# The first attention batch of a fused attention and MLP kernel: two squares a unit on GpSimd, QK and transposes interleaved singly, Z and PV of unit 2 summed beside its exponentials

## Chip, cores, metric

One core of a Trainium2 chip. The metric is the device time of one execution in microseconds (us), as the median of several runs. The rounds ran on different chips; a ratio always compares a kernel with the kernel before in the same rounds. A profile is one execution; its span is 1.7 to 1.9 us shorter than the device time of the same run.

## The reference, cut to what matters

```python
# q, k, v: [8 batches, 12 heads, 448, 64] float32
def rmsnorm(x, g):
    return x / np.sqrt(np.mean(x * x, axis=-1, keepdims=True) + 1e-06) * g
scores = np.matmul(rmsnorm(q, g_q), rmsnorm(k, g_k).transpose(0, 1, 3, 2)) / np.sqrt(64)
attn = softmax(scores)                      # with the row maximum taken off
x = heads_side_by_side(np.matmul(attn, v))  # [3584, 768]
h = x @ w_in                                # [768, 2048]
out = np.maximum(0.01 * h, h) @ w_out       # [2048, 768]
```

## The kernel before

The work is cut into 24 units of four heads; three units make a batch. Each unit goes through the same steps:

- squares of q and k (`prep_sq` on ScalarE or `prep_sqp` on GpSimd), their sums (`prep_ssq`, VectorE), 1/rms as Ln and Exp (`prep_rinv`, ScalarE), the norm (`prep_norm`, VectorE) and the transposes (`prep_tr`, TensorE with a copy by VectorE);
- scores S^T for seven key tiles (`qk`), the first of which gives the shift of the exponent (`shift_max` on VectorE, `shift_mm` on TensorE and VectorE), and seven exponentials (`ex`, ScalarE);
- Z, the sum of the exponentials (`zsum`), and PV (`pv`), 28 matmuls each, then 1/Z as Ln and Exp (`zinv`) and their product (`xmul`).

The MLP of a batch (`moe1`, `moe2`) needs all three units. It waits in a queue, from which `fill` takes work for TensorE between the later units' steps. So from unit 3 on there is MLP work to fill TensorE with; in units 0 to 2 there is none. The parts that the change touches:

```python
def zsum(u):
    s = st[u]
    s["zt"] = slot()
    for t in range(NS):                       # 7 key tiles, 4 matmuls each
        for r in range(2):
            for a in range(2):
                nc.tensor.matmul(s["zt"][64 * a:64 * a + 64, r, 0:S], ones16[64 * r:64 * r + 64],
                                 s["et"][64 * r:64 * r + 64, t, a], start=(t == 0), stop=(t == NS - 1))
# pv(u): the same loop with v for ones16, into two banks
# ... cut ...
for u in range(3):
    ex(u)
    if u == 0:
        prep_ssq(1)
    prep_rinv(u + 1)
    if u > 0:
        zinv(u - 1)
    prep_sq(u + 2, ALL, (0 if u == 0 else 1,))
    prep_norm(u + 1)
    if u > 0:
        xmul(u - 1)
    # ... loads cut ...
    prep_qg(u + 2, nc.gpsimd)
    prep_sqp(u + 3, (0,))
    qk(u, STEPS[1]); ex(u)
    prep_ssq(u + 2)
    if u == 0:
        qk(u, STEPS[2]); ex(u); qk(u, STEPS[3]); ex(u)
        for ti in range(2):
            prep_tr(u + 1, ti, VV)
        score0(u + 1); shift_max(u + 1)
    else:
        for ti in range(2):
            prep_tr(u + 1, ti, VV)
        qk(u, STEPS[2]); ex(u)
        score0(u + 1); shift_max(u + 1)
        qk(u, STEPS[3]); ex(u)
    shift_mm(u + 1)
    zsum(u)
    pv(u)
```

The softmax here doesn't subtract the row's maximum and nothing guards it: scores larger than these inputs give would overflow.

## Time and profile before

| | before |
|---|---|
| median | 459.26 us (459.0 to 459.46, 3 runs) |
| span of the profile | 458.0 us |
| TensorE busy to 55.9 us | 35.7 of 55.9 us |
| TensorE busy after it | 396.2 of 402.1 us |

Two lines of the page of the kernel before: busy time by engine, with the share of the span, and the clock granted to TensorE in 40 slices of 11.45 us, in tenths of full speed.

```profile
PE 431.9 (94%) x3840; PEld 223.5 (49%) x3840; DVE 205.9 (45%) x320; ACT 314.4 (69%) x446; POOL 95.9 (21%) x74
...
PEclk9567899999999999999999999999999999999999
```

The first line says that TensorE is the busy engine, but it averages two stages. The second marks the stage in which it is not: slices 2 to 5 have a reduced clock, and in the same slices TensorE's own row, which opens the prediction, reads only 4, 6, 7 and 6 tenths busy. An array at half clock is called cold below, one at full clock warm.

### The profile page before, as it was taken

How to read it: one execution, taken by the hardware profiler on the slowest of the kernel's cores; microseconds unless marked ns; L12 is line 12 of the kernel's file. 1: busy time of each engine (PE TensorE's matmuls, PEld its weight loads, DVE VectorE, ACT ScalarE, POOL GpSimd, SP SyncE). 2: the span in 40 equal slices, each digit the busy share in tenths (PEclk: the TensorE clock that was granted, in tenths of full speed). 3: DMA queues.
4: the chain of work that ended last, by engine and by line, in shares of the span. 5: the costliest groups of instructions: out<-in, count | busy, mean ns of one | idle time of the engine just before them, and what ended most of it. 6: DMA issues, size and time to landing. Idle time of an engine off the chain costs nothing.

```text
span 458.0 us, 8922 instructions
## 1 busy us (share of the span) xinstructions
PE 431.9 (94%) x3840; PEld 223.5 (49%) x3840; DVE 205.9 (45%) x320; ACT 314.4 (69%) x446; POOL 95.9 (21%) x74
## 2 busy tenths in 40 slices
PE   7467699999999999999999999999999999999995
PEld 6133244554445544554455544554455544555563
DVE  3766564555434733645434634654444631311021
ACT  4858688768876679858876679767876678544300
POOL 3954331330230330331130330331130200000000
PEclk9567899999999999999999999999999999999999
DMA  8999997545625734644644733654633330021022
GB/s 283 191 236 228 163 225 152 134 97 157 142 43 161 182 73 106 142 97 147 142 74 138 176 76 101 142 106 139 142 55 76 76 76 0 2 70 36 0 69 70
DMA packets 62508, 54.13 MB, mean 118 GB/s; under 512 B 36868, under 2 KB 57348, under 8 KB 62468
## 3 DMA queue, kind: packets, MB, share of 16 engines
q1 hardware_dynamic: 52192, 41.76, 33.6%
q0 software_dynamic: 10272, 11.80, 17.1%
q8 instruction: 30, 0.49, 0.4%
q14 instruction: 10, 0.08, 0.0%
q10 hardware_dynamic: 4, 0.00, 0.0%
HBM read 45.61 MB, written 11.01 MB: 124 GB/s over the span
## 4 chain that ended last, share of the span: by engine, by line
PE 88%; ACT 5%; DVE 4%; DMA 1%; issue 1%; ACTq 0%; DVEq 0%
PE op L280 32%; PE hps L265 31%; PE sT L235 8%; PE sT L175 8%; PE pv L250 7%; ACT et L194 3%; DVE ssq L135 1%; PE warm L350 1%; PE pb L219 1%; DVE pm L207 1%; PE tp L155 1%; ACT gt L267 1%; DMA grow<-in_g_k_dram 1%; DVE qkT L156 1%; ACT sq L122 1%; DVE xt L259 1%
## 5 line engine op out<-in xcount | busy, mean ns | idle before, releaser
L194 ACT ACTIVATE et<-sT,eb 128x896 f16<-128x896 f32 x165 | 158.0, 1009 | 37.6 <-PE sT L175 35.0
L265 PE MATMUL hps<-xt,win 128*128 128x448 f16 x768 | 153.1, 353 | 0.8 <-ACT et L192 0.8
L280 PE MATMUL op<-wout,gt 128*128 128x384 f16 x896 | 153.3, 326 | 0.0
L280 PEld LDWEIGHTS <-gt 128*128 128x128 f16 x896 | 84.6, 98 | 63.3 <-issue 10.9
L130 POOL TENSOR_TENSOR qg<-rq,ggb 128x896 f32<-128x896 f32 (+2 forms) x25 | 63.9, 2559 | 236.5 <-DVE n L147 232.3
L265 PEld LDWEIGHTS <-win 128*128 128x128 f16 x768 | 72.2, 98 | 75.0 <-issue 10.9
L267 ACT ACTIVATE gt<-hps 128x448 f16<-128x448 f32 x128 | 65.6, 548 | 25.2 <-PE hps L265 24.6
L284 DVE COPY ost<-op 128x384 f32<-128x384 f32 x56 | 31.0, 556 | 89.9 <-PE op L280 89.8
L147 DVE TENSOR_TENSOR n<-qg,rinv 128x896 f16<-128x896 f32 (+2 forms) x25 | 26.5, 1063 | 81.9 <-ACT rinv L141 44.2
L175 PE MATMUL sT<-qkT 64*64 64x448 f16 x660 | 51.6, 370 | 7.5 <-ACT et L194 6.8
L135 DVE TENSOR_REDUCE ssq<-sq 128x14 f32<-128x896 f32 (+2 forms) x49 | 49.9, 1059 | 5.1 <-ACT sq L122 5.1
L241 ACT ACTIVATE rz<-sT 128x896 f32<-128x896 f32 x24 | 22.0, 917 | 42.0 <-PE sT L235 42.0
L235 PE MATMUL sT<-et,ones 64*64 64x448 f16 x672 | 39.9, 378 | 0.6 <-ACT et L194 0.5
L250 PE MATMUL pv<-et,vt 64*64 64x448 f16 x672 | 37.9, 363 | 0.0
L175 PEld LDWEIGHTS <-qkT 64*64 64x64 f16 x672 | 14.5, 106 | 45.9 <-issue 38.9
L259 DVE TENSOR_TENSOR xt<-pv,rz 128x448 f16<-128x448 f32 x48 | 27.7, 619 | 9.7 <-ACT rz L242 8.6
L212 DVE TENSOR_REDUCE sT<-sT 128x1 f32<-128x896 f32 x21 | 23.0, 1096 | 19.6 <-PE sT L175 19.5
L235 PEld LDWEIGHTS <-ones 64*64 64x64 f16 x672 | 20.6, 113 | 16.1 <-issue 7.4
L250 PEld LDWEIGHTS <-vt 64*64 64x64 f16 x672 | 20.9, 112 | 13.5 <-issue 2.7
L147 DVE TENSOR_TENSOR n<-rk,rinv 128x896 f16<-128x896 f32 (+2 forms) x25 | 26.2, 1047 | 0.0
L242 ACT ACTIVATE rz<-rz 128x896 f32<-128x896 f32 x24 | 22.8, 949 | 0.8
L122 ACT ACTIVATE sq<-rk 128x896 f32<-128x896 f32 x23 | 21.6, 940 | 0.2 <-DMA rk<-in_k_dram 0.2
(48 smaller groups left out, 136.4 us busy)
## 6 DMA issues: line engine op xcount, KB each, us to landing
rq<-in_q_dram SPq DMA_DIRECT2D x24, 448.0 KB, 6.2
rk<-in_k_dram SPq DMA_DIRECT2D x24, 448.0 KB, 6.4
out_dram<-ost SPq DMA_DIRECT2D x56, 192.0 KB, 2.7
vt<-in_v_dram POOLq DMA_DIRECT2D x24, 224.0 KB, 6.0
win<-in_moe_w_in_dram POOLq DMA_DIRECT2D x8, 384.0 KB, 12.3
wout<-in_moe_w_out_dram POOLq DMA_DIRECT2D x2, 1536.0 KB, 18.4
qkT<-n SPq DMA_TRANSPOSE x19, 4.0
grow<-in_g_q_dram ACTq DMA_DIRECT2D x1, 0.2 KB
```

The lines of the kernel that those rows point to most:

```text
L130: eng.tensor_tensor(buf(u, "qg")[:, :, c[0]:c[1]], raw[u][0][:, :, c[0]:c[1]], ggb[:, None, None, :].broadcast_to([P, 2, n, D]), op=ALU.mult)
L135: nc.vector.tensor_reduce(buf(u, "ssq")[:, ti, :, c[0]:c[1]], buf(u, "sq")[:, ti, :, c[0]:c[1]], axis=AXL.X, op=ALU.add)
L147: nc.vector.tensor_tensor(buf(u, "n16")[:, ti, c[0]:c[1]].rearrange("p s a d -> p a s d"), src[:, :, c[0]:c[1]], buf(u, "rinv")[:, ti, :, ...
L175: nc.tensor.matmul(banks[a][64 * r:64 * r + 64, 0:S].rearrange("p (t x) -> p t x", t=NS), kT(u, r, a, t), qT(u, r, a), start=True, stop=True)
L194: nc.scalar.activation(s["et"][:, t], sT[:, :, 0:S], AF.Exp, bias=s["eb"], scale=1.0)
L235: nc.tensor.matmul(s["zt"][64 * a:64 * a + 64, r, 0:S], ones16[64 * r:64 * r + 64], s["et"][64 * r:64 * r + 64, t, a], start=(t == 0), sto ...
L250: nc.tensor.matmul(s["pv"][r][64 * a:64 * a + 64, 0:S], vts[u % NV][64 * r:64 * r + 64, a, t], s["et"][64 * r:64 * r + 64, t, a], start=(t ...
L259: nc.vector.tensor_tensor(xts[b][:, g, r], s["pv"][r][:, 0:S], s["rz"][:, r], op=ALU.mult)
L265: nc.tensor.matmul(hps[:, 0:S], win16[:, kt // 2, kt % 2, ts(ft, P)], xt[:, kt // 2, kt % 2], start=(kt == 0), stop=(kt == KT - 1))
L267: nc.scalar.activation(gt[:, ft, ds(S * (b % 2), S)], hps[:, 0:S], AF.Prelu, bias=0.0, scale=1.0, alpha=0.01)
L280: nc.tensor.matmul(op2[:, 0:HC], gt[:, ft, ts(t, P)], wout16[:, ft, ds(HC * half, HC)], start=(ft == 0), stop=(ft == FT - 1))
L284: nc.vector.tensor_copy(ost[0][:, ds(HC * half, HC)], op2[:, 0:HC])
```

## The change

The intent is to shorten the first batch, in which TensorE waits, so that the stage which it saturates starts earlier. The diff, cut to its core (left out are the new arguments of `zsum`, `zinv` and `pv`, calls moved with them, the square of unit 5 that leaves ScalarE, and the load of the output weights, now issued in unit 1 instead of unit 2):

```diff
-        for x in range(20): warm-up matmul
+        warm(32)                                   # before the product of the two gains
         ...
-        vcopy(ggb, gps[:, 0:D])
-        for x in range(44): warm-up matmul
+        warm(28)
         ...
+        acopy(ggb, gps[:, 0:D])
         ...
+        prep_sq(1, ALL, (0,))                      # ahead of unit 0's copies on ScalarE
         ...
+        prep_ssq(1, ALL, (0,))                     # ahead of unit 0's maximum on VectorE
         qk(0, STEPS[0])
-        prep_sq(1)
+        prep_sq(1, ALL, (1,))
 
         for u in range(3):
+            n = u + 1
             ex(u)
             if u == 0:
-                prep_ssq(1)
+                prep_ssq(n, ALL, (1,))
             ...
-            prep_sq(u + 2, ALL, (0 if u == 0 else 1,))
             ...
-            prep_sqp(u + 3, (0,))
+            prep_sqp(u + 3)                        # both squares on GpSimd
             ...
             ex(u)
-            prep_ssq(u + 2)
-            ... (u == 0: QK 3 to 6, then both transposes; else transposes, QK 3, 4, shift, QK 5, 6)
-            shift_mm(u + 1)
-            zsum(u)
-            pv(u)
+            if u > 0:
+                prep_tr(n, 0, VV)
+                prep_tr(n, 1, VV)
+                xmul(u - 1)
+            qk(u, STEPS[2])
+            ex(u)
+            if u == 0:
+                prep_tr(n, 0, VV)
+            qk(u, (5,))
+            ex(u)
+            if u == 0:
+                prep_tr(n, 1, VV)
+                qk(u, (6,)); ex(u); prep_sq(2, ALL, (0,)); score0(n); shift_max(n); shift_mm(n)
+            elif u == 1:
+                score0(n); shift_max(n); qk(u, (6,)); ex(u); shift_mm(n)
+            else:
+                qk(u, (6,)); ex(u)
+            if u < 2:
+                zsum_slot(u); pv(u)
+                prep_ssq(u + 2)                    # now behind the shift
+            else:
+                prep_ssq(u + 2)
+                st[u]["zt"] = [aux([P, 512], FP32, "zt") for r in range(2)]
+                zsum(u, 0, 5)                      # while exponentials 5 and 6 run
+                pv(u, 0, 5)
+                qk(n, STEPS[0])
+                zsum(u, 5, NS)
+                pv(u, 5, NS)
+                zinv(u)                            # in two halves
+                shift_max(n)
+                xmul(u)
+                push_moe1(0); push_moe2(0); queue.pop(0)[1]()
+                shift_mm(n)
+                ex(n)
```

More of the change, by code (lines that the diff above doesn't have):

```diff
@@ L227, with zsum, zsum_slot @@
     xts = {}
-    def zsum(u):
+    def zsum(u, t0=0, t1=NS):
         s = st[u]
-        s["zt"] = slot()
-        for t in range(NS):
+        for t in range(t0, t1):
             for r in range(2):
                 for a in range(2):
-                    nc.tensor.matmul(s["zt"][64 * a:64 * a + 64, r, 0:S], ones16[64 * r:64 * r + 64],
+                    nc.tensor.matmul(s["zt"][r][64 * a:64 * a + 64, 0:S], ones16[64 * r:64 * r + 64],
                                      s["et"][64 * r:64 * r + 64, t, a], start=(t == 0), stop=(t == NS - 1))
+    def zsum_slot(u):
+        s = st[u]
+        s["zslot"] = slot()
+        s["zt"] = [s["zslot"][:, r] for r in range(2)]
+        zsum(u)
     def zinv(u):
@@ L240, in zinv, with pv @@
         s["rz"] = zpool.tile([P, 2, S], FP32, tag="rz", name="rz")
-        nc.scalar.activation(s["rz"], s["zt"][:, :, 0:S], AF.Ln)
-        nc.scalar.activation(s["rz"], s["rz"], AF.Exp, bias=0.0, scale=-1.0)
-    def pv(u):
+        if "zslot" in s:
+            nc.scalar.activation(s["rz"], s["zslot"][:, :, 0:S], AF.Ln)
+            nc.scalar.activation(s["rz"], s["rz"], AF.Exp, bias=0.0, scale=-1.0)
+        else:
+            for r in range(2):
+                nc.scalar.activation(s["rz"][:, r], s["zt"][r][:, 0:S], AF.Ln)
+                nc.scalar.activation(s["rz"][:, r], s["rz"][:, r], AF.Exp, bias=0.0, scale=-1.0)
+    def pv(u, t0=0, t1=NS):
         s = st[u]
-        s["pv"] = [aux([P, 512], FP32, "pv") for r in range(2)]
-        for t in range(NS):
+        if t0 == 0:
+            s["pv"] = [aux([P, 512], FP32, "pv") for r in range(2)]
+        for t in range(t0, t1):
             for r in range(2):
@@ L328, with warm @@
     VV = ((ALL, vcopy),)
-    def attend(u):
-        zsum(u)
-        pv(u)
-        zinv(u)
+    def warm(n):
+        for x in range(n):
+            nc.tensor.matmul(wbank[:, 0:P], onesp, onesp, start=True, stop=True)
     with tc.manual_schedule():
@@ L341 @@
         load(2)
+        gps = aux([P, 512], FP32, "gps")
+        wbank = aux([P, 512], FP32, "warm")
+        warm(32)
         nc.vector.scalar_tensor_tensor(grow[:, 0], grow[:, 0], 0.125, grow[:, 1], op0=ALU.mult, op1=ALU.mult)
-        gps = aux([P, 512], FP32, "gps")
-        warm = aux([P, 512], FP32, "warm")
-        for x in range(20):
-            nc.tensor.matmul(warm[:, 0:P], onesp, onesp, start=True, stop=True)
         nc.tensor.matmul(gps[:, 0:D], one32, grow[:, 0], start=True, stop=True)
-        vcopy(ggb, gps[:, 0:D])
-        for x in range(44):
-            nc.tensor.matmul(warm[:, 0:P], onesp, onesp, start=True, stop=True)
+        warm(28)
         prep_sq(0, CA, (0,))
         prep_sq(0, CB, (0,))
+        acopy(ggb, gps[:, 0:D])
         prep_sq(0, ALL, (1,))
@@ L366 @@
         prep_norm(0, K0, (1,))
+        prep_norm(0, K1, (1,))
         tpk = aux([P, NS, P], FP16, "tp")
@@ L374 @@
         trk(K0, vcopy)
-        prep_norm(0, K1, (1,))
+        prep_ssq(1, ALL, (0,))
         qk(0, STEPS[0])
-        prep_sq(1)
+        prep_sq(1, ALL, (1,))
         trk(K1, acopy)
@@ L388 @@
         for u in range(3):
+            n = u + 1
             ex(u)
             if u == 0:
-                prep_ssq(1)
-            prep_rinv(u + 1)
+                prep_ssq(n, ALL, (1,))
+            prep_rinv(n)
             if u > 0:
                 zinv(u - 1)
-            prep_sq(u + 2, ALL, (0 if u == 0 else 1,))
-            prep_norm(u + 1)
-            if u > 0:
-                xmul(u - 1)
+            prep_norm(n)
             load(u + 4)
-            gate(u + 1)
+            gate(n)
             prep_qg(u + 2, nc.gpsimd)
-            prep_sqp(u + 3, (0,))
+            prep_sqp(u + 3)
             load_v(u + 3)
@@ L405 @@
                 load_w_in(1024, 1024)
-            if u == 2:
+            if u == 1:
                 for f in range(2):
@@ L410 @@
             ex(u)
-            prep_ssq(u + 2)
-            if u == 0:
-                qk(u, STEPS[2])
-                ex(u)
-                qk(u, STEPS[3])
+            if u > 0:
[4 more added lines that the diff above has]
+            ex(u)
+            if u == 0:
+                prep_tr(n, 0, VV)
[3 more added lines that the diff above has]
+                prep_tr(n, 1, VV)
+                qk(u, (6,))
+                ex(u)
+                prep_sq(2, ALL, (0,))
+                score0(n)
+                shift_max(n)
+                shift_mm(n)
+            elif u == 1:
+                score0(n)
+                shift_max(n)
+                qk(u, (6,))
@@ L416 @@
                 ex(u)
-                for ti in range(2):
-                    prep_tr(u + 1, ti, VV)
-                score0(u + 1)
-                shift_max(u + 1)
-            else:
-                for ti in range(2):
-                    prep_tr(u + 1, ti, VV)
-                qk(u, STEPS[2])
+                shift_mm(n)
+            else:
+                qk(u, (6,))
                 ex(u)
-                score0(u + 1)
-                shift_max(u + 1)
-                qk(u, STEPS[3])
-                ex(u)
@@ L430 @@
-            shift_mm(u + 1)
-            zsum(u)
-            pv(u)
+            if u < 2:
+                zsum_slot(u)
+                pv(u)
+                prep_ssq(u + 2)
[8 more added lines that the diff above has]
+                zinv(u)
+                shift_max(n)
+                xmul(u)
+                push_moe1(0)
+                push_moe2(0)
+                queue.pop(0)[1]()
+                shift_mm(n)
+                ex(n)
@@ L434 @@
         for u in range(3, NU):
             for d in range(4):
-                if u > 3 or d > 0:
+                if d > 0 or u > 3:
                     qk(u, STEPS[d])
-                if d == 0 and u > 3:
-                    shift_max(u)
-                    zsum(u - 1)
-                    pv(u - 1)
-                    shift_mm(u)
-                    zinv(u - 1)
-                if u == 3 and d == 0:
-                    zinv(u - 1)
-                ex(u)
+                    if d == 0:
+                        shift_max(u)
+                        zsum_slot(u - 1)
+                        pv(u - 1)
+                        shift_mm(u)
+                        zinv(u - 1)
+                    ex(u)
@@ L447 @@
                 if d == 0:
-                    xmul(u - 1)
                     if u == 3:
-                        push_moe1(0)
-                        push_moe2(0)
                         prep_rinv(4)
@@ L454 @@
                         gate(4)
+                    else:
+                        xmul(u - 1)
                     if u + 4 < NU:
@@ L468 @@
                         prep_tr(4, ti, VV)
-                    prep_sq(5, ALL, (1,))
                 if u + 2 < NU:
@@ L477 @@
                 fill(u, d)
-        attend(NU - 1)
+        zsum_slot(NU - 1)
+        pv(NU - 1)
+        zinv(NU - 1)
         xmul(NU - 1)
```

## The prediction

> **What bounds the kernel now.** I read the page's rows of busy tenths first, to find out where the span is lost, then the busy time by stretch, then the waits and the timeline of the stretch that loses.
>
> ```profile
> PE   7467699999999999999999999999999999999995
> ACT  4858688768876679858876679767876678544300
> ```
>
> A slice is 11.45 us. TensorE is saturated from the sixth slice on and ragged in the first five. Busy time by stretch, cut where the clock changes, puts numbers on that (columns after the length: PE, PEld, DVE, ACT, POOL busy, then the clock granted):
>
> ```profile
> 13.30:30.10 16.80, 9.23 (x80) 3.99 (x83) 10.77 (x19) 10.25 (x17) 13.21 (x15) 0.50 0.98 216
> 30.10:36.90 6.80, 4.12 (x70) 2.26 (x63) 6.02 (x9) 6.28 (x8) 4.59 (x4) 0.99 1.15 225
> 36.90:43.80 6.90, 5.50 (x63) 2.64 (x65) 3.83 (x8) 5.76 (x9) 0.71 (x2) 0.51 0.96 219
> 43.80:50.70 6.90, 3.19 (x51) 1.66 (x47) 5.81 (x10) 5.79 (x7) 5.64 (x5) 0.99 0.75 180
> 50.70:54.00 3.30, 3.30 (x40) 1.58 (x44) 0.46 (x2) 0.67 (x2) 0.00 (x0) 0.50 0.95 143
> 55.90:110.00 54.10, 53.23 (x489) 26.84 (x488) 30.27 (x44) 43.25 (x63) 13.62 (x9) 1.00 0.77 166
> 110.00:458.00 348.00, 342.96 (x2973) 175.68 (x2969) 141.77 (x216) 233.47 (x332) 52.71 (x29) 1.00 0.40 94
> ```
>
> From 55.9 us on, PE is idle for 0.9 + 5.0 us of 402, most of it the tail. So the span is about "time of the first MLP matmul" plus 402 us of TensorE work that the diff leaves alone. What the change can gain is an earlier start of that saturated stage. Before it, nothing is saturated: the limit is one chain that goes round ScalarE, VectorE and TensorE. ScalarE's timeline shows its holes:
>
> ```profile
> 14.54 1.01 ACT L194 ACTIVATE et<-sT,eb 128x896 f16<-128x896 f32 x1 [0.50 <-DVE eb L222]
> 16.52 0.32 ACT L140 ACTIVATE uu<-ssq,eps_t 128x28 f32<-128x28 f32 x1 [0.98 <-DVE ssq L135]
> 17.00 0.93 ACT L122 ACTIVATE sq<-rq 128x896 f32<-128x896 f32 x1
> 17.84 5.48 ACT L194 ACTIVATE et<-sT,eb 128x896 f16<-128x896 f32 x6
> 27.77 1.16 ACT L192 ACTIVATE et<-s,eb 128x448 f16<-128x448 f32 x2 [4.44 <-DVE eb L222]
> 39.13 1.16 ACT L192 ACTIVATE et<-s,eb 128x448 f16<-128x448 f32 x2 [0.46 <-DVE eb L222]
> 48.93 1.91 ACT L194 ACTIVATE et<-sT,eb 128x896 f16<-128x896 f32 x2 [1.03 <-PE sT L175]
> 53.46 0.92 ACT L241 ACTIVATE rz<-sT 128x896 f32<-128x896 f32 x1 [2.63 <-PE sT L235]
> ```
>
> First exponentials of units 0, 1, 2 start at 14.54, 27.77, 39.13; unit 3's at 55.27. The 4.44 us hole is unit 1's shift: in unit 0 the transposes of unit 1 come after the last QK, so copies, score tile and maximum run while ScalarE has nothing left. The 2.63 us hole is Z of unit 2, started only after unit 3's shift, on a cold array. TensorE's side of that end:
>
> ```profile
> 50.60 2.81 PE L235 MATMUL sT<-et,ones 64*64 64x448 f16 x28
> 53.20 1.93 PE L250 MATMUL pv<-et,vt 64*64 64x448 f16 x28
> 55.94 3.57 PE L265 MATMUL hps<-xt,win 128*128 128x448 f16 x18 [0.81 <-ACT et L192]
> ```
>
> 28 Z matmuls take 2.81 us here and 1.5 us at full clock (68.9 us).
>
> **What the Trainium skill says.** "GPSIMD Engine Reference", section 4.1, calls GpSimd about 2x slower than VectorE on two-input elementwise work. The trace agrees in kind: a square of 128x896 takes 1.67 us there against 0.94 on ScalarE. It matters only if GpSimd's row fills up. "TensorE: Matmul & The Clock Gate", Part 1, says that the clock is halved or full, judged over free-running windows of about 3.4 us. The trace agrees: 0.50 and 1.00, with changes near 30.1, 36.9, 43.8, 50.7 and 54.0, all multiples of 3.4 us apart. The same part says that ScalarE's and VectorE's queues are strictly in order; hence a reduction placed behind a shift waits for it even if its data came early. No run here tests that by itself.
>
> **The change part by part.** I carry the chain forward with the durations of the trace: square on ScalarE 0.94, sum of squares on VectorE 1.04, rinv pair 0.58, exponential 0.92 start to start, norm pair 2.18, tp copy 0.6, Ln+Exp of Z 1.87, shift from the score tile to the bias 3.2 (24.49 to 27.68).
>
> *Prologue.* 60 warm-up matmuls instead of 64, 32 of them before the gain product instead of 20. The second string (44 at 0.107) ended at 9.91 and held unit 0's transposes, whose input was ready near 8.1. Now it ends by 8.2. But a square of unit 1 now sits on ScalarE before the copies (8.05 to 9.0), so the first copy starts at 9.0 (was 10.18), the first QK at 10.55 (was 11.7). A sum of squares ahead of the maximum on VectorE delays that to 11.45 (was 12.24). First exponential: 13.7. **Gain 0.8.**
>
> *Unit 0.* Only one sum of squares remains between shift and rinv (-1.0) and the square of unit 2 leaves the place before the second exponential (-0.94): exponential 1 starts at 15.4 (was 17.84). QK and transposes alternate, which costs ScalarE about 0.7 us of waits on a cold array (QK 0.59, seven transposes 0.85). The last exponential ends at 21.7, the score tile of unit 1 starts at 20.8 (was 24.49), the bias comes at 24.0. The moved square fills 0.94 us of the hole. Unit 1 starts at 24.0 (was 27.77). **Gain 3.8.**
>
> *Unit 1.* Its ScalarE square goes (-0.94). Against it, the sums of squares of unit 2 now come after the bias: 24.0 to 26.05, so rinv waits 0.95, and Z's Ln starts at 26.65 instead of about when Z is ready. Exponential 1 at 28.5 (was 32.60). The score tile stands behind QK 5, which waits for exponential 3: 31.6; the bias is ready at 34.95, and ScalarE waits 1 us where it waited 0.46. **Gain 4.1**: this unit nearly breaks even.
>
> *Unit 2.* Sums of squares again behind the bias (35.0 to 37.05), rinv, Ln/Exp to 39.5; PV of unit 1 ends at 40.2 if cold, 38.9 if not. Six exponentials from 40.5, none waiting for transposes any more (the 1.03 hole goes): end 46.0 (was 50.84). Gain there 4.8.
>
> *Tail of unit 2.* 40 of the 56 matmuls of Z and PV now start after exponential 4 (44.2) instead of after the last one and a shift: 2.0 us at full clock, 3.7 if cold for one window. Then QK of unit 3, 16 matmuls, and Ln/Exp in halves: four at about 0.53 = 2.1, 0.25 more than whole. At full clock: first part 46.2, QK 46.6, Z 47.0, Ln/Exp 49.1, second product 49.7, first MLP group done 50.1. Cold: 51.8. Before, that group ended at 57.25. **Gain 5.5 to 7.2.**
>
> *After it.* Unit 3's exponential stands behind the first MLP activation and a shift that waits for the MLP group: 50.9 against 50.1 for the group, where before it was ahead of it (55.27 against 57.25). ScalarE starts this stage some 2 us behind, but loses the square of unit 5 (0.94) and had 2 us of waits between 57 and 66. Three more MLP groups (1.13 each) feed TensorE meanwhile. I expect at most 0.5 us of it on TensorE. GpSimd: two squares and one product a unit, 2 x 1.67 + 2.08 = 5.4, plus at most 3.3 of issuing, in a period of 11 us: it stays hidden. Output weights are issued some 12 us earlier, but behind the input weights on one queue, and are wanted only at 81 us.
>
> Sum: 5.5 to 7.2, mean 6.3, less 0.4 for ScalarE's lag: **about 5.9 us**, 459.26 - 5.9 = **453.4 us**.
>
> **The rivals.** (1) *VectorE's order takes the gain back.* Sums of squares behind the shift (2.05 us each in units 1 and 2) delay rinv, norms, transposes and the next score tile. The waits speak for it: ScalarE's and VectorE's chain is the bound in this stage, and two moves lengthen it. Then units 1 and 2 lose what unit 0 won, and the time is 456 to 457. Against it: each reduction runs while TensorE is still at Z and PV. (2) *The clock.* Alternating small groups on TensorE may leave the array cold throughout: each Z and PV pair then costs 5.6 us instead of 2.8. That makes 455; a warm array from 40 us on makes 452. (3) *The MLP start is limited by something else*: weights landing (12 us from issue to landing, issued in time even before) or squares on GpSimd arriving late. Squares of unit 3 wait for unit 1's norm gate, then 2.08 + 3.34 us: ready near 23, wanted at 35. So against; it would make 458. (4) *All holes close* and the saturated stage starts at ScalarE's own bound: 8.9 us of work a unit after 13.7, or near 47. That would be 449, the only path to over 2%; the shift chains (3.2 us each) stand in its way.
>
> **Range and chances.** 2% is 9.2 us, more than my best case of 7.2. Slower by 2% would take 15 us of new waits. The saturated stage passes the gain on whole. 8 in 10: 450.9 to 456.3. Faster by over 2%: 0.07; within: 0.92; slower: 0.01.
>
> **What would show it.** Unit firsts on ScalarE's timeline at about 13.7, 24.0, 35.0 and 51 (14.54, 27.77, 39.13, 55.27 before); the 4.44 us wait for the bias down to about 1.5; waits of rinv for sums of squares of about 1 us in units 1 and 2; the first activation of an MLP group near 50 to 52 (57.27 before); PE idle after that unchanged at about 6 us. I am wrong if the MLP starts early but the span does not follow (a new wait in units 3 to 6), or if unit 2's Z does not start before its last exponential.

## The result and the profile after

| | median | runs | ratio to before |
|---|---|---|---|
| before | 459.31 us | 459.0 to 459.46 (4) | |
| changed | 451.47 us | 450.32 to 452.29 (4) | 0.9828 (0.9806 to 0.9851) |
| changed, again, on another occasion | 450.98 us | 450.06 to 452.23 (4) | 0.9818 (0.9799 to 0.9837) |

A ratio is the mean time of one kernel's runs over that of the other's of the same rounds, so it is not quite the ratio of the medians. The gain is 7.8 us by the first medians, against 5.9 predicted: inside the range, near its lower end in time. Note the spread. The changed kernel's eight runs lie between 450.06 and 452.29 us. The four of the kernel before lie within 0.5 us here, but all its 27 runs in the later rounds lie between 458.5 and 460.29: it is steadier, though by less than these four suggest.

The page of the changed kernel, the rows that answer to those of before (busy tenths of TensorE and ScalarE, granted clock; a slice is now 11.2 us):

```profile
PE   7577899999999999999999999999999999999995
...
ACT  6878788867964788767964788758875687544300
...
PEclk9689999999999999999999999999999999999999
```

TensorE's fifth slice reads 8 where it read 6, and the clock is reduced in two slices (the second and third) where it was reduced in four. ScalarE's timeline of the changed kernel, the rows that answer to those in the prediction:

```profile
13.63 1.01 ACT L194 ACTIVATE et<-sT,eb 128x896 f16<-128x896 f32 x1 [0.82 <-DVE eb L222]
...
15.10 3.69 ACT L194 ACTIVATE et<-sT,eb 128x896 f16<-128x896 f32 x4
...
23.60 1.16 ACT L192 ACTIVATE et<-s,eb 128x448 f16<-128x448 f32 x2 [1.35 <-DVE eb L222]
25.53 0.32 ACT L140 ACTIVATE uu<-ssq,eps_t 128x28 f32<-128x28 f32 x1 [0.76 <-DVE ssq L135]
...
27.80 5.48 ACT L194 ACTIVATE et<-sT,eb 128x896 f16<-128x896 f32 x6
33.76 1.16 ACT L192 ACTIVATE et<-s,eb 128x448 f16<-128x448 f32 x2 [0.47 <-DVE eb L222]
...
38.01 5.48 ACT L194 ACTIVATE et<-sT,eb 128x896 f16<-128x896 f32 x6
44.62 0.54 ACT L251 ACTIVATE rz<-zt 128x448 f32<-128x448 f32 x1 [1.13 <-PE zt L234]
...
47.91 0.54 ACT L278 ACTIVATE gt<-hps 128x448 f16<-128x448 f32 x1 [1.10 <-PE hps L276]
```

The bracket is ScalarE's idle time just ahead of the row and what ended it. The wait of 4.44 us for unit 1's shift is 1.35 us; the one of 1.03 us in unit 2 is gone (six exponentials now run on end); the one of 2.63 us for Z is 1.13. Two waits of about 0.8 us for sums of squares are new (0.76 here, 0.83 in unit 2). The last row is the first MLP activation, 57.27 us before.

TensorE in the kernel before, Z of unit 1:

```profile
38.50 2.83 PE L235 MATMUL sT<-et,ones 64*64 64x448 f16 x28
```

TensorE in the changed kernel, Z and PV of unit 1, then the first part of Z of unit 2 and the first MLP group:

```profile
33.12 1.52 PE L234 MATMUL sT<-et,ones 64*64 64x448 f16 x28
34.47 1.49 PE L261 MATMUL pv<-et,vt 64*64 64x448 f16 x28
...
41.94 1.14 PE L234 MATMUL zt<-et,ones 64*64 64x448 f16 x20
...
45.22 0.92 PE L276 MATMUL hps<-xt,win 128*128 128x448 f16 x4 [0.25 <-ACT rz L251]
```

Here the 28 Z matmuls of unit 1 take 1.52 us. In the kernel before they took 2.83 at half clock, as did PV of unit 1. The window from the first MLP activation to the end, before and changed (columns: length; PE, PEld, DVE, ACT, POOL busy; clock; DMA):

```profile
57.27:458.00 400.73, 394.86 (x3452) 201.84 (x3450) 171.11 (x258) 275.78 (x391) 66.33 (x38) 1.00 0.45 104
```

```profile
47.91:448.60 400.69, 394.97 (x3453) 201.95 (x3450) 171.70 (x260) 276.14 (x393) 66.36 (x38) 1.00 0.46 105
```

The two lengths agree to 0.04 us. All of the span's 9.4 us in this pair of profiles was won before that point, and none was lost after it. The pair is a favourable one: the profiled run of the kernel before took 459.77 us, that of the changed one 450.32, its fastest of four.

### The profile page after: what moved, and what is told of

Same layout as the page of the kernel before. It is cut to its first block, busy times and chain, and to the rows that moved or that the text cites. A ratio compares the mean times of both kernels' runs of the same rounds, so it can differ in the third digit from the quotient of the medians.

```text
span 448.6 us, 8910 instructions
## 1 busy us (share of the span) xinstructions
PE 427.7 (95%) x3836; PEld 221.7 (49%) x3836; DVE 205.6 (46%) x317; ACT 311.9 (70%) x445; POOL 100.8 (22%) x77
## 4 chain that ended last, share of the span: by engine, by line
PE 88%; ACT 6%; DVE 3%; DMA 1%; issue 0%; SPq 0%
PE op L291 33%; PE hps L276 32%; PE sT L175 8%; PE pv L261 6%; PE sT L234 6%; ACT et L194 4%; DMA rq<-in_q_dram 1%; DVE ssq L135 1%; PE pb L219 1%; PE tp L155 1%; DVE pm L207 1%; ACT rz L248 0%; ACT rz L247 0%; ACT gt L278 0%; PE zt L234 0%
## 5 line engine op out<-in xcount | busy, mean ns | idle before, releaser
L175 PE MATMUL sT<-qkT 64*64 64x448 f16 x664 | 52.7, 371 | 6.8 <-ACT et L194 5.2
L247 ACT ACTIVATE rz<-sT 128x896 f32<-128x896 f32 x23 | 21.1, 916 | 38.6 <-PE sT L234 38.6
L234 PE MATMUL sT<-et,ones 64*64 64x448 f16 x644 | 35.2, 355 | 0.6 <-ACT et L194 0.5
L212 DVE TENSOR_REDUCE sT<-sT 128x1 f32<-128x896 f32 x22 | 24.1, 1095 | 19.2 <-PE sT L175 19.1
L248 ACT ACTIVATE rz<-rz 128x896 f32<-128x896 f32 x23 | 21.8, 949 | 0.7
L122 ACT ACTIVATE sq<-rq 128x896 f32<-128x896 f32 (+2 forms) x22 | 19.8, 906 | 1.3 <-DMA rq<-in_q_dram 1.3
```

The lines of the kernel that those rows point to most:

```text
L175: nc.tensor.matmul(banks[a][64 * r:64 * r + 64, 0:S].rearrange("p (t x) -> p t x", t=NS), kT(u, r, a, t), qT(u, r, a), start=True, stop=True)
L234: nc.tensor.matmul(s["zt"][r][64 * a:64 * a + 64, 0:S], ones16[64 * r:64 * r + 64], s["et"][64 * r:64 * r + 64, t, a], start=(t == 0), sto ...
```

## The experiments

Two theories about the size. **A, the parts add**: each part is worth the wait that it removes from the chain. **B, the clock**: much of the gain, and the spread of the changed kernel, depends on whether TensorE is at full or half clock when it comes to Z and PV. They can both hold; the first four runs weigh the parts, the rest the clock and what lies beyond the change. The changed kernel itself was timed again only in the rounds of runs 5 to 8; the others are held against it by their ratios to the kernel before. The first MLP activation and the end of each profile, in us:

| kernel | first exponential | first MLP activation | span | span less MLP activation |
|---|---|---|---|---|
| before | 14.54 | 57.27 | 458.0 | 400.7 |
| changed | 13.63 | 47.91 | 448.6 | 400.7 |
| changed, again | 13.33 | 49.87 | 450.5 | 400.6 |
| tail undone | 14.21 | 51.05 | 451.7 | 400.7 |
| order undone | 13.80 | 49.55 | 450.2 | 400.7 |
| squares undone | 13.69 | 49.91 | 450.5 | 400.6 |
| prologue undone | 14.15 | 50.26 | 450.9 | 400.6 |
| tail alone | 14.34 | 53.89 | 454.5 | 400.6 |
| dummies in before | 14.29 | 55.43 | 456.1 | 400.7 |
| dummies in units 0, 1 of changed | 13.83 | 50.02 | 450.6 | 400.6 |
| sums spread | 14.36 | 48.43 | 449.0 | 400.6 |
| spread and MLP prefilled | 13.44 | 47.90 | 449.0 | 401.1 |
| all | 14.24 | 47.33 | 448.4 | 401.1 |
| dummies in unit 2 of changed | 13.99 | 48.58 | 449.2 | 400.6 |

The last column is the main result in one place: over the twelve profiles of eleven kernels that leave the MLP's own order alone, the time from the first MLP activation to the end varies by 0.1 us. The two kernels that move MLP work itself (401.1) are the exceptions.

### 1. The changed kernel with its tail undone

```diff
-            elif u == 1:
+            else:
                 score0(n); shift_max(n); qk(u, (6,)); ex(u); shift_mm(n)
-            ... (sums of unit 2 beside its exponentials)
+            zsum_slot(u); pv(u); prep_ssq(u + 2)
 # at unit 3, step 0:
+                        zinv(2); ex(3); xmul(2); push_moe1(0); push_moe2(0)
```

> The changed kernel with the end of unit 2 as before: unit 3's score tile and shift first, Z and PV of unit 2 whole and after its last exponential, Ln and Exp whole, no MLP group ahead of unit 3's shift. Theory A (the tail is worth what the two traces show between the end of unit 2's exponentials and the end of the first MLP group: 57.25 - 50.84 = 6.4 us before, 47.9 - 43.5 = 4.4 us after): 2.0 us are lost, about 453.5 us. Rival (most of those 2.0 us were the cold array, 2.81 us against 1.5 for 28 Z matmuls, and the array is warm here anyway): at most 0.7 us are lost, about 452, and Z takes about 1.5 us.

Measured 453.13 us (452.65 to 453.51), ratio 0.9868 (0.9853 to 0.9883). Against 0.9823, the middle of the changed kernel's two ratios, that is 0.0045 x 459.3 = 2.1 us: theory A's figure. The rival's condition did not hold in the profiled run. TensorE of this kernel, Z and PV of unit 2:

```profile
44.17 2.83 PE L234 MATMUL sT<-et,ones 64*64 64x448 f16 x28
46.78 2.56 PE L261 MATMUL pv<-et,vt 64*64 64x448 f16 x28
```

The array was at half clock from 42.1 to 48.9 us. From the end of unit 2's exponentials (44.28) to the first MLP activation (51.05) it takes 6.8 us, against 4.4 in the first profile of the changed kernel, whose tail was warm, and 5.7 in the second (run 8), whose tail was cold too, though only to 45.1. So with both cold the profiles show 1.1 us for the tail, and the rest of the 2.1 may be the clock. What it is worth at full clock isn't shown by this run.

### 2. The changed kernel with unit 0's order undone

```diff
-            if u == 0:
-                prep_tr(n, 0, VV)
             qk(u, (5,)); ex(u)
             if u == 0:
-                prep_tr(n, 1, VV)
                 qk(u, (6,)); ex(u)
                 prep_sq(2, ALL, (0,))
+                prep_tr(n, 0, VV)
+                prep_tr(n, 1, VV)
```

> The changed kernel with both transposes of unit 1 after unit 0's last QK, as before. Theory A (the score tile of unit 1 follows the transposes, so it starts later by two groups of cold transposes and their copies, less the 0.6 us of exponentials' waits): unit 1's first exponential comes 1.5 to 2 us later than 23.60, and the time is about 453.2 us. Rival (the wait is hidden, because rinv of unit 2 waits for sums of squares anyway): under 0.5 us lost, about 451.8.

Measured 452.10 us (451.45 to 453.57), ratio 0.9851 (0.983 to 0.9871): 1.3 us by the ratios, between the two figures. ScalarE's timeline of this kernel:

```profile
25.19 1.16 ACT L192 ACTIVATE et<-s,eb 128x448 f16<-128x448 f32 x2 [3.60 <-DVE eb L222]
```

The wait for unit 1's shift is back (3.60 us), and unit 1's first exponential comes 1.6 us later than in the changed kernel, 1.4 of it after allowing for the later start of this run (13.80 against 13.63). Against the second profile of the changed kernel, which like this one was cold through all of unit 0, it is 1.2 us (25.19 less 23.56, less 0.47 for the start). The mechanism is theory A's, its size 1.2 to 1.4 and not 1.5 to 2.

### 3. The changed kernel with the squares undone

```diff
-            prep_sqp(u + 3)
+            prep_sqp(u + 3, (0,))
             if u > 0:
                 zinv(u - 1)
+                prep_sq(u + 2, ALL, (1,))
 # at unit 3, step 1:
+                    prep_sq(5, ALL, (1,))
```

> The changed kernel with the second square of units 3, 4 and 5 on ScalarE again, in the places it had. Theory A (in units 1 and 2 it stands between Ln/Exp and the exponentials on the chain): 0.9 us lost in each of units 1 and 2, none in unit 3, about 453.2 us. Rival (ScalarE has waits of 0.8 us in each unit that take it up): at most 0.5 us lost, about 451.8.

Measured 452.95 us (452.29 to 454.84), ratio 0.9871 (0.9847 to 0.9896): 2.2 us by the ratios, of which theory A expected 1.8. ScalarE's timeline in unit 1:

```profile
28.12 0.93 ACT L122 ACTIVATE sq<-rk 128x896 f32<-128x896 f32 x1
28.96 5.48 ACT L194 ACTIVATE et<-sT,eb 128x896 f16<-128x896 f32 x6
```

The second exponential of unit 1 comes 5.04 us after its first (28.96 less 23.92), where the changed kernel has 4.20; unit 2 shows 5.10 against 4.25. ScalarE's waits of 0.8 us do not take the square up, because they end ahead of it. But not all of unit 1's 0.84 us is the square's. PV of unit 0 was partly cold in this run, and TensorE came to the next QK only here:

```profile
28.05 0.54 PE L175 MATMUL sT<-qkT 64*64 64x448 f16 x8
```

In the second profile of the changed kernel QK starts at 28.05 too, and the exponential follows at 28.47 without any square in the way. So the square cost some 0.5 us in unit 1 (28.96 less 28.47, an estimate) and 0.85 in unit 2: 1.3 us in the profile, which is the fastest of the four runs, of the 2.2 in the ratios.

### 4. The changed kernel with the prologue undone

The prologue of before put back: 20 and 44 warm-up matmuls, gains copied by VectorE, both squares of unit 1 behind the first QK, and both sums of unit 1 behind unit 0's shift.

> The changed kernel with the prologue of before (44 warm-up matmuls after the gain product, unit 1's squares and sums of squares where they were). Theory A (first exponential 0.9 us later, and a second sum of squares between shift and rinv, 1.05 us more, both on the chain): exponentials from the second on 1.9 us later, about 453.3 us. Rival (the waits in unit 0 take the second part up): about 452.3.

Measured 453.68 us (452.65 to 454.69), ratio 0.9888 (0.9871 to 0.9905): 3.0 us by the ratios, more than either expected. In the profile, the second exponential starts at 16.62 us against 15.10, 1.5 later, and unit 1 at 25.33 against 23.60, 1.7 later. Only 0.5 of it is there at the first exponential (14.15 against 13.63), so the moved sums matter more than the shorter string of warm-up matmuls. In this profile the first MLP activation is 2.3 us later (50.26 against 47.91): after the 1.7, unit 2's second exponential waits 0.45 us for a QK behind a cold PV, for this run had half clock from 32.9 to 39.7 us. It was the fastest of the four (452.65 us); what the others lost beyond it is not accounted for.

The four parts undone one by one come to 2.1 + 1.3 + 2.2 + 3.0 = 8.6 us, and the whole change to 0.0177 x 459.3 = 8.1. With intervals of 0.7 to 1.1 us either way on each, and one reference common to all four, the two figures are known to agree only within about 3 us: that the parts add is compatible with this, not shown by it (run 5 will find 3.0 us for the tail alone).

### 5. The kernel before with the tail alone

The kernel before with only the end of unit 2 changed, as in the diff above.

> The kernel before with only the end of unit 2 changed (Z and PV of unit 2 begun after its fifth exponential, Ln and Exp in halves, the first MLP group ahead of unit 3's shift). Theory A (the parts add, and the tail is worth 2.0 us): about 457.3 us. Rival 1 (the array's clock decides: begun at 47.9 us the sums run at full clock, which the trace of before grants until 50.7): 3 us or more, 456. Rival 2 (the tail alone is worth nothing once the halves cost 0.25 us and the MLP group waits for Ln and Exp): 459.

Measured 456.40 us (456.06 to 456.68), ratio 0.9934 (0.9921 to 0.9947): 3.0 us. That is rival 1's figure, but not only for its reason. Exponentials end at 49.47 us and the first MLP activation comes 4.42 us later, against 6.43 us before: the 2.0 us that theory A named. The other microsecond is the hole of 1.03 us in unit 2, which closes with the tail, since unit 3's score tile no longer stands between QK 4 and QK 5. Theory A forgot that. The sums did run at full clock, which this profile grants from 43.6 us on.

### 6. The kernel before with dummy matmuls

```diff
     def shift_mm(u, dummies=0):
         pb = aux([P, 512], FP32, "pb")
+        for x in range(dummies):           # 16, 12, 12 in units 0, 1, 2
+            nc.tensor.matmul(pb[:, P:2 * P], onesp, onesp, start=True, stop=True)
         nc.tensor.matmul(pb[:, 0:P], onesp, s["dg"], start=True, stop=True)
```

> The kernel before with 16, 12 and 12 dummy 128x128 matmuls ahead of the shift's matmul in units 0, 1 and 2, in time in which TensorE waits for the maximum anyway. Theory (the clock matters to this stage: Z and PV of units 0, 1 and 2 take 2.81 and 1.9 to 2.83 us cold, 1.5 and 1.5 at full clock, and each pair ends on the chain to the next QK or to the MLP): 2 to 3.5 us gained, about 456.5. Rival (TensorE isn't on the chain in this stage, or the dummies do not change the clock): within 0.7 us of 459.3.

Measured 457.97 us (457.01 to 458.69), ratio 0.9967 (0.9952 to 0.9981). Work that computes nothing saves 1.5 us: clear of zero, but below the 2 to 3.5 expected. The profile shows why it may be less: the clock was still at half from 12.9 to 30.0, 36.8 to 40.2 and 47.1 to 50.5 us. TensorE of this kernel, Z of unit 2:

```profile
49.67 1.90 PE L237 MATMUL sT<-et,ones 64*64 64x448 f16 x28
```

1.90 us, between the 2.81 us of before and 1.5. Unit 1's Z was still cold (2.49), its PV not (1.49 against 2.83).

### 7. The changed kernel with dummies in units 0 and 1

> The changed kernel with 16 and 10 such dummies in units 0 and 1. Theory (in some runs the array is cold in units 1 and 2, and those are the slow ones of 450.3 to 452.3 us): a median near 450 and a narrower spread. Rival (the spread has another cause, or the dummies delay the shift): 451.4 or more, with the same spread.

Measured 452.45 us (451.44 to 453.14), ratio 0.9847 (0.983 to 0.9864), against 0.9818 for the changed kernel in the same rounds. So it is no better, and the spread is 1.7 us. The expectation failed. The window ahead of the tail, and the first part of Z of unit 2 in this kernel's profile:

```profile
38.80:42.30 3.50, 1.76 (x23) 0.87 (x27) 3.37 (x7) 3.50 (x5) 3.22 (x3) 1.00 1.18 224
```

```profile
42.37 2.11 PE L236 MATMUL zt<-et,ones 64*64 64x448 f16 x20
```

Units 1 and 2 were at full clock up to 42.3 us. Then, after a stretch in which TensorE was busy 1.76 of 3.50 us with no gap above 0.52, the clock fell just as the tail began, and 20 Z matmuls took 2.11 us instead of 1.14. By this profile the dummies were in the wrong place; run 12 tries another.

### 8. The changed kernel once more

> The changed kernel once more, for the spread of its runs on the same chip and for a second profile. If the clock's free-running phase makes the spread, then this profile shows other stretches at half clock than the first (which was cold at 10.0 to 20.1 and 23.8 to 26.9 us), and time and mean clock go together: each 0.01 of mean clock missing below 50 us counts about 1 us or less. Otherwise the same stretches appear and the time differs with them unchanged.

Measured 450.98 us (450.06 to 452.23). The profiled run was the slowest of these (452.23), and its profile differs from the first one in the clock. TensorE, to be held against the rows of the first profile above:

```profile
42.76 2.13 PE L234 MATMUL zt<-et,ones 64*64 64x448 f16 x20
44.62 1.36 PE L261 MATMUL pv<-et,vt 64*64 64x448 f16 x20
...
47.18 0.92 PE L276 MATMUL hps<-xt,win 128*128 128x448 f16 x4 [0.25 <-ACT rz L251]
```

Half clock stood from 41.7 to 45.0 us, and from 11.0 to 28.0 without a break. The tail, from the end of the exponentials to the first MLP activation, took 49.87 - 44.18 = 5.69 us; in the first profile, 47.91 - 43.49 = 4.42. Another 0.6 us came from QK of unit 1, which came late behind a cold PV. ScalarE's timeline shows the wait, which the first profile does not have:

```profile
28.47 5.49 ACT L194 ACTIVATE et<-sT,eb 128x896 f16<-128x896 f32 x6 [0.61 <-PE sT L175]
```

Together that is the 1.9 us between the two spans. The other expectation, that a run's mean clock foretells its time, failed: the runs of 450.06 and 451.26 us both had 0.982. The mean over the span says nothing about where the slow stretch lies. In the kernel before, though, mean clock and time do go together: of its 27 later runs the eight fastest (458.5 to 459.08 us) all have 0.972, and the three slowest (460.05 to 460.29) all have 0.966.

### 9. Sums of unit 2 spread

```diff
             qk(u, (5,)); ex(u)
+            if u == 2:
+                prep_ssq(4); zt = two banks
+                zsum(2, 0, 2); pv(2, 0, 2)
             qk(u, (6,)); ex(u)
-                zsum(u, 0, 5); pv(u, 0, 5); qk(n, STEPS[0]); zsum(u, 5, NS); pv(u, 5, NS)
+                zsum(u, 2, 5); pv(u, 2, 5); qk(n, STEPS[0])
+                zsum(u, 5, 6); pv(u, 5, 6); zsum(u, 6, NS); pv(u, 6, NS)
```

> The changed kernel with Z and PV of unit 2 begun two exponentials earlier and spread: key tiles 0 and 1 after QK 5, 2 to 4 after QK 6, 5 and 6 as they come. Theory (what differs between two profiles of the changed kernel, 47.91 and 49.87 us for the first MLP activation, is the clock: the array is half idle in unit 2's exponentials and in some runs falls to half clock just before the sums): sums among the exponentials shorten what is left after the last one from 36 to 8 matmuls, so the first activation comes about 0.5 us earlier in a warm run and 1.5 or more earlier than in a cold one: median 450.0, spread under 1.5 us. Rival (the spread comes from elsewhere): a median within 0.4 of the changed kernel's 451.2 and the same spread of 2 us.

Measured 450.23 us (450.21 to 450.84), ratio 0.9806 (0.9792 to 0.982): as expected, with a spread of 0.6 us instead of 2.2. Four runs are few for a spread, but runs 10 and 11, which have the same spread sums, also kept within 1.0 and 0.2 us. The tail takes 48.43 - 44.53 = 3.90 us, 0.5 less than the changed kernel's warm one. But this profile started late, and the reason is a cost of the change that the prediction missed. ScalarE's timeline:

```profile
9.04 0.95 ACT L122 ACTIVATE sq<-rq 128x896 f32<-128x896 f32 x1 [0.89 <-DMA rq<-in_q_dram]
9.89 0.57 ACT L156 COPY qkT<-tp 128x512 f16<-128x512 f16 x1
```

The square of unit 1 that was moved ahead of unit 0's copies waits 0.89 us for unit 1's q to land, and the copies wait behind it. Over the profiles of kernels with this prologue the wait was 0, 0, 0, 0 and 0.22, 0.46, 0.53, 0.83, 0.89, 1.00 us, and the first exponential came between 13.33 and 14.36 us, on the whole the later the longer the wait.

### 10. Spread, and MLP matmuls in the tail's wait

```diff
+                hs = slot()                     # one tile, two banks
+                hps = [hs[:, 0], hs[:, 1], aux([P, 512], FP32, "hps")]
+                for ft in range(3): first four of six matmuls of MLP group ft
                 shift_max(n); xmul(u)
-                queue.pop(0)[1]()
+                for ft in range(3): the fifth; then for ft in range(3): the sixth and the activation
                 shift_mm(n); ex(n)
```

> As e8_spread, and the first three MLP groups have their first four of six matmuls, which need only units 0 and 1, run in the 2.5 us in which TensorE waits for Ln, Exp and the product of unit 2. Theory (once past the first batch the span is TensorE's work, so any matmul moved into a wait ahead of it comes off the span): 8 matmuls more than now run in that wait, 8 x 0.19 = 1.5 us off e8_spread, about 448.6 us. Rival (ScalarE, which starts the stage late, then holds TensorE back): under 0.5 us off.

Measured 450.96 us (450.69 to 451.72), ratio 0.9822 (0.9808 to 0.9837): no gain over the spread alone. The theory failed and its rival held. TensorE's waits of this kernel from 45 to 60 us:

```profile
PE tp L155 <- DVE n L147: 1.0, 2, 0.6
PE sT L275 <- ACT gt L279: 0.6, 1, 0.6
```

Columns: total us, times, longest. Two groups share one tile, so the sixth matmul of the second waited for the first one's activation (0.6 us). And three activations now stand on ScalarE ahead of unit 4's rinv, which starts at 50.63 us against 49.92, relative to the first MLP activation 2.7 us against 1.5; norms and transposes of unit 4 follow it, and TensorE waits 1.0 us for them. The 8 x 0.19 = 1.5 us moved into the wait were given back as two new ones.

### 11. All of it, with sums of squares ahead of the shift

```diff
             prep_norm(n)
+            if u == 0:
+                prep_ssq(2, ALL, (1,))
             ...
                 zsum_slot(u)
+                qk(n, (1,))                        # ahead of PV
                 pv(u)
-                prep_ssq(u + 2)
+                prep_ssq(2, ALL, (0,)), prep_ssq(3, ALL, (0,))  if u == 0 else  prep_ssq(3, ALL, (1,))
```

> As e9_spread_prefill, and the sums of squares that came in early are reduced before the shift instead of behind it (one of two for units 2 and 3), and the first QK of units 1 and 2 goes ahead of PV. Theory (the reductions behind the shift are what rinv waits for, 0.76 and 0.83 us, and Ln/Exp and the exponentials follow it): 0.7 us off in each of units 1 and 2, about 447.2 us. Rival (the exponentials are then held by TensorE, whose norms, transposes and PV come no earlier): under 0.4 us off.

Measured 450.14 us (450.00 to 450.17), ratio 0.9801 (0.9787 to 0.9814). From the first exponential to the last of unit 2 it takes 29.15 us, where run 9 took 30.17 and run 10 30.52. So 1.0 to 1.4 us were won in units 1 and 2, and the time fell by 0.8 against run 10: between the theory's 1.4 and the rival's 0.4, and the 447.2 us expected, which counted on run 10's 448.6, were missed by 3. Part of what was won can be the clock: this profile is warm from 28.2 us on, those of runs 9 and 10 were cold once more for 3.4 us. ScalarE's timeline in unit 1 shows no wait for sums of squares any more:

```profile
25.52 0.32 ACT L140 ACTIVATE uu<-ssq,eps_t 128x28 f32<-128x28 f32 x1
```

This kernel is the fastest measured by median and the steadiest (0.2 us over four runs). Its interval overlaps those of the changed kernel, so that it beats it by about 1 us isn't shown, nor that it beats run 9 (450.23).

### 12. The changed kernel with dummies in unit 2

> The changed kernel with 6 dummy 128x128 matmuls behind QK 3/4 and 6 behind QK 5 of unit 2, where TensorE waits 0.5 us for each exponential. Theory (clock): the tail's 20 first Z matmuls take 1.14 us in every profile, never 2.1; the slow runs go, median about 450.4. Rival (dummies do not change when the clock falls, or delay QK): 451.2 or more.

Measured 450.91 us (450.32 to 451.81), ratio 0.982 (0.9803 to 0.9836). In the profile the 20 first Z matmuls took 1.14 us, as the theory has it, but the median isn't below the changed kernel's by more than the noise, and one profile cannot show that the clock is full in every run. Inconclusive. So that the clock makes the whole spread of the changed kernel is argued from its two profiles, not shown.

## Why the prediction was right, and where its sizes were off

**The frame held.** It read the span as "time of the first MLP matmul, plus TensorE work that the diff leaves alone", and said that the gain passes on whole. Measured: 400.7 us after the first MLP activation in both kernels.

**The size came out low.** The measured 7.8 us, and 8.4 by the ratio of the second occasion, lie above the prediction's own best case of 7.2, and 450.98 us is less than 0.1 above the lower end of the range. The table shows where the excess arose.

**The chain, step by step** (us; the two profiles of the changed kernel):

| | before | predicted | changed | again |
|---|---|---|---|---|
| first exponential, unit 0 | 14.54 | 13.7 | 13.63 | 13.33 |
| second exponential, unit 0 | 17.84 | 15.4 | 15.10 | 14.80 |
| first exponential, unit 1 | 27.77 | 24.0 | 23.60 | 23.56 |
| second exponential, unit 1 | 32.60 | 28.5 | 27.80 | 28.47 |
| first exponential, unit 2 | 39.13 | 35.0 | 33.76 | 34.44 |
| last exponential of unit 2 ends | 50.84 | 46.0 | 43.49 | 44.18 |
| first MLP activation | 57.27 | 50.1 to 51.8 | 47.91 | 49.87 |

*Prologue and unit 0*: right to 0.4 us, in its parts as well (warm-up string, moved sums, transposes between QKs), as runs 2 and 4 show. Missed: the moved square waits for its data in some runs, up to 1.0 us.

*Unit 1*: the new wait of rinv was put at 0.95 us and measured 0.76. The shift was sized 3.2 us from a cold trace; from the score tile (30.82) to the bias (33.72) it took 2.9 here.

*Unit 2*: this is the term that was mis-sized. The prediction put the end of PV of unit 1 at 40.2 us cold, 38.9 not, and took the cold figure on to the exponentials' end at 46.0. Measured: PV ended at 36.0, because the bias came 1.2 us earlier (33.72 for 34.95) and because Z and PV took 2.8 us together, not the 5.6 of a cold array. Its other figure, 38.9, doesn't follow from its own numbers either: 40.2 less 5.6 plus 2.8 is 37.4, ahead of the 39.5 at which it has ScalarE free. ScalarE's own Ln and Exp were then the bound, and the second exponential came at 38.01 us instead of 40.5. In both profiles of the changed kernel unit 1's Z and PV ran at full clock. The clock was named as rival 2, with both signs; the sum took the cold figure. Of the 2.5 us by which the exponentials ended early, 0.4 had come from unit 0, 0.8 from unit 1 (half of it the shorter shift), and 1.25 arose here.

*Tail*: 4.1 us predicted from the end of the exponentials at full clock (46.0 to 50.1), 4.42 measured; cold 5.8 (46.0 to 51.8), measured 5.69. Which one a run gets depends on the clock, which the array kept through unit 2 in the first profile and lost there in the second, at 41.7 us.

*After it*: 0.4 us were taken off for ScalarE's lag; nothing was lost there. In run 10, which adds two activations to that lag, TensorE does wait.

*GpSimd*: hidden, as said. Two squares and a product a unit; up to 48 us its largest wait in total is its own gate (5.5 us in four), and from 10 to 48 us no instruction is shown to wait for it. What the prediction set beside the skill's "about 2x slower than VectorE" was a time of ScalarE's; VectorE's own product of this size, `n` (written as float16), takes 1.09 us where GpSimd's `qg` takes 2.08.

**The rivals**: the first (VectorE's order takes the gain back) is real but small, about 0.8 us a unit; run 11 removes its waits. The third (weights or squares late) shows nowhere in the profiles. The fourth (all holes close) would have made 449; even run 11, which closes three more waits, comes only to 450.1.

## What to carry to other kernels

Find the point from which one engine is saturated to the end, and read a change ahead of it as a change of that point alone: here its distance to the end stayed within 0.1 us over eleven kernels. Size TensorE's work in a ragged stage at both clocks and ask which of them a shorter stage will get, for closing the waits here also raised the clock (its mean over the span is 0.966 to 0.972 in the 27 later runs of the kernel before, 0.974 to 0.983 in those of the changed one), and a stage that hovers between the two gives each run another time. Work put into an idle engine's wait is only won if the engine that consumes it next isn't late already.

## What the Trainium skill lacked or had wrong

- "TensorE: Matmul & The Clock Gate", Part 1, ties the fall to half clock to an idle window of about 3.4 us, and its closing table to gaps of over about 3 us. Here the clock fell after a stretch of that length with TensorE busy 1.76 of 3.50 us and no gap above 0.52 us (run 7), and stayed full after one with 2.11 of 3.43 us (the first profile of the changed kernel). Where a window begins is inferred from when the clock changed. So a half-busy TensorE can lose its clock too. The same part does report a kernel whose clock oscillates because of frequent short idles, but gives no share of busy time, and the share alone does not decide: in the profile of run 4 the clock stayed full after 1.63 of 3.41 us busy (22.64 to 26.05) and fell after 1.96 of 3.41 (29.47 to 32.88).
- The same page, Part 1, puts the ramp's cost under 1% of a typical span. The differences that go with the clock here are smaller than that. It says that the number of slow matmuls varies from run to run, but not what this does to the time: two profiles of one kernel differ by 1.9 us of 450 with the place of the slow stretches, as much as a part of the change is worth, and 40 dummy matmuls in the kernel before save 1.5 us.
- The same page, Part 1, warns that clock events in a trace can be unreliable, but not that the granted clock may read 1.00 ahead of its first change: in the kernel before it reads 1.00 to 13 us, while the 44 warm-up matmuls from 5.18 us on take 4.73 us, 0.107 each, where 28 of the same took 1.74 us, 0.062 each, in the second profile of the changed kernel.
- "GPSIMD Engine Reference", section 3.1, gives one figure for two-input work, about 2.6 cycles an element. On 128x896 float32, a square (both inputs the same tile) takes 1.67 us and a product with a broadcast operand 2.08 us; at the page's 1.2 GHz that is 2.2 and 2.8 cycles, an estimate by its clock (and the profile's times for GpSimd are rough).
